# A fifth expert slot from the early plan: attention, a dense layer and routed experts on one Trainium2 core

## The chip, the cores and the metric

The kernel runs on one core of a Trainium2 chip. The metric is the device time of one execution in microseconds (us); a kernel is given by the median of several executions. The engines are named as in the profile: PE (matrix products), DVE and ACT (vector and scalar work), POOL (here mostly the issue of indirect and padding DMAs), SP (here only the issue of DMAs, in the order of its queue; SPq in the rows).

## The reference

Three layers follow one another, in float32.

```python
# 1. gated linear attention, B=4, H=8, S=768, D=48
f = sigmoid(f_logit)
state = f[t] * state + outer(k[t], v[t]);  y[t] = q[t] @ state
# 2. dense layer on the 3072 tokens (width 384, hidden 2048)
h = x @ w_in;  g = softplus(h);  x = g @ w_out
# 3. one expert of eight for each token (hidden 1024)
logits = x @ w_gate + modality_bias[modality_id]
e_idx = argmax(logits);  gate_w = softmax(logits)[e_idx]
out[mask_e] = gate_w * (relu(x[mask_e] @ w1[e]) @ w2[e])
```

How many tokens go to each expert is known only when the second layer is done. On the reference's own inputs the eight counts are 20, 327, 542, 487, 219, 1097, 167 and 213; of the first seven groups of 384 tokens alone they are 17, 281, 476, 430, 193, 956, 154 and 181.

## The kernel before

**First part.** Attention and the dense layer run together over eight groups of 384 tokens (`ffn`). At the end of each group `route1` and `route2` choose the expert of each token and scatter its row into a DRAM buffer `xs`, where each expert has a region of its own, in the order of arrival. After the eighth group, `tails` and `pad_rows` write 256 padding rows behind each expert's last row: eight DMAs on POOL's queue.

**Expert slots.** The third layer runs over a list `seq` of slots, each of one expert: twelve full slots of 256 tokens (number 0 to 11), then one "pair" slot of two half experts of 64 tokens (12), then two slots of 128 tokens (13 and 14). Which expert and which rows a slot takes is decided on the device. `plan_first` counts after seven groups and gives out whole blocks of 256 rows that are complete by then, up to `NPRE` of them. `plan_rest` counts after all eight groups, takes off what the first plan used, and gives out `NA` more full slots, two halves for the pair, and 128-token slots; with the full ones these make the `NSTAT` entries of the fixed list. Only if the plan needs more entries than `NSTAT` a further branch behind the list is entered (up to `NREST` entries, `more`).

**One slot.** `m_fetch` brings what a slot needs while the slot before it computes: two register loads on SP read expert and row from the plan (L994 and L982), one DMA reads the rows (`m_load`, L984, tile `xr`), and eight DMAs (L1008) read the weights in chunks of 128x768 into tiles `raw`, in the order w1, w2, w1, w2 and so on. ACT casts each chunk into a high part (L1009), DVE makes the low part (L1010). The DMA of the rows stands behind the first two chunks. `m_T` turns the rows (L1097 to L1100). `m_up` makes eight hidden tiles: nine products each (L1115), then ACT's relu `hh` (L1117) and DVE's low part `hl` (L1118). `m_down` makes two output tiles of 24 products each (L1138), ACT scales (L1147) and POOL scatters the rows into `out` (L1148). Full slots take turns in two sets of weight tiles, so slot 4 writes into the tiles of slot 2; there are six `raw` tiles and three `xr` tiles, so slot 4's rows go into the tile of slot 1, which is free when slot 1's two output scatters are through.

**Order.** Each engine works off one fixed list in order. A list scheduler makes the lists when the kernel is built, mostly by program order. The steps `final`, `route2`, `ready` (tails and padding) and `then` (the second plan) are hung onto slots 0, 1, 1 and 2:

```python
seq = [("first", i, 2) for i in range(NPRE)] + [("rest", i, 2 if i < NA else 1) for i in range(NSTAT)]
seq.insert(PAIRAT, ("pair", 0, 1))
more = [("rest", i, 1) for i in range(NSTAT, NREST)]
m_slots(seq, {(0, 3): final, (1, 2): lambda: route2(NG - 1), (1, 4): ready, (2, 2): then, (6, 3): limits})
# in m_load: the first plan's rows don't wait for the last group's scatters (scat) and the padding (pads)
for other in scat + pads:
    if where == "first":
        tc.declare_no_dep(ins, other, reason="rows of the groups ahead")
    else:
        after(ins, other)
```

Of the kernel before, what the change touches and what calls it, by code (L numbers as in the profile page):

```python
# [24 lines left out]
NB = 16  # L25
SLOT = 256
CAP = NT + SLOT
NPRE = 4
NA = 8
NREST = 17  # L30
NSTAT = 10
HALF = 64
PAIRAT = 12
LEAN = 16
# [17 lines left out]
def moe_chain(ctx, tc, qT, kT, fT, vp, w_in, w_out, mod, w_gate, mbias, w1, w2, out):  # L52
# [682 lines left out]

    used = cp.tile([NREST, 8], F32, name="used")

    def pick(nm, num, w, offs):


        end, beg, oh, tmp, off = (cp.tile([NREST, w], F32, name=f"{x}{nm}") for x in ("end", "beg", "soh", "stmp", "off"))
        sel, row = (cp.tile([NREST, 1], F32, name=f"{x}{nm}") for x in ("sel", "row"))
        woff, roff = (cp.tile([NREST, 1], I32, name=f"{x}{nm}") for x in ("woff", "roff"))
        nc.vector.tensor_tensor_scan(end, num, zer[:, 0:w], 0.0, op0=ALU.add, op1=ALU.add)
        nc.vector.tensor_tensor(beg, end, num, op=ALU.subtract)
        nc.vector.tensor_scalar(tmp, beg, snum[:, 0:1], None, op0=ALU.is_le)
        nc.vector.scalar_tensor_tensor(oh, end, snum[:, 0:1], tmp, op0=ALU.is_gt, op1=ALU.mult)
        nc.vector.tensor_tensor(tmp, oh, etab[:, 0:w], op=ALU.mult)
        nc.vector.tensor_reduce(sel, tmp, axis=AX.X, op=ALU.add)
        nc.vector.tensor_copy(woff, sel)  # L750

        nc.vector.scalar_tensor_tensor(off, beg, snum[:, 0:1], step[:, 0:w], op0=ALU.subtract, op1=ALU.mult)
        nc.vector.tensor_tensor(tmp, offs, off, op=ALU.subtract)
        nc.vector.tensor_tensor(tmp, tmp, oh, op=ALU.mult)
        nc.vector.tensor_reduce(row, tmp, axis=AX.X, op=ALU.add)
        nc.vector.tensor_scalar(roff, row, float(PADROW), None, op0=ALU.add)
        return woff, roff, beg, end

    def counts(sh, add):
        p = ps_r.tile([128, 512], F32, tag="r", name="r")  # L760
        nc.tensor.matmul(p[:, 0:8], onesb, runb, start=True, stop=True)
        cf, ci = cp.tile([NREST, 8], F32, name=f"cf{sh}"), cp.tile([NREST, 8], I32, name=f"ci{sh}")
        nc.vector.tensor_copy(cf, p[0:NREST, 0:8])
        nc.vector.tensor_scalar(ci, cf, float(add), None, op0=ALU.add)
# [3 lines left out]
    def taken(dst, beg, num, n):  # L768

        nc.vector.tensor_scalar(dst, beg, -1.0, float(n), op0=ALU.mult, op1=ALU.add)  # L770
        nc.vector.tensor_scalar(dst, dst, 0.0, None, op0=ALU.max)
        nc.vector.tensor_tensor(dst, dst, num, op=ALU.min)

    def plan_first():

        _, ci, _ = counts(8, 0)
        num = cp.tile([NREST, 8], F32, name="num0")
        nc.vector.tensor_copy(num, ci)
        woff, roff, beg, _ = pick("0", num, 8, rows0[:, 0:8])
        taken(used, beg, num, NPRE)  # L780
        return woff, roff
# [30 lines left out]
    def plan_rest():  # L812
# [12 lines left out]
        nc.vector.tensor_tensor(beg, end, num, op=ALU.subtract)  # L825
        taken(n16[:, 0:8], beg, num, NA)
        nc.vector.tensor_tensor(num, used, n16[:, 0:8], op=ALU.add)
# [11 lines left out]
    def limits():  # L839
# [4 lines left out]
        nc.vector.tensor_copy(nsl[:, 0:1], end)  # L844
        nc.vector.tensor_scalar(far, end, float(-NSTAT), 0.0, op0=ALU.add, op1=ALU.max)
        nc.vector.tensor_reduce(flm, fl, axis=AX.X, op=ALU.max)
# [34 lines left out]
    def at(s, f):  # L881
        extra.setdefault(s, []).append(f)
# [98 lines left out]
    def m_load(s, where, i, n):  # L981
        ro = nc.sync.value_load(plans[where][1][i:i + 1, 0:1], min_val=0, max_val=PADROW)  # L982
        xr = xrp.tile([128, 2, RW], F32, tag="xr", name="xr")[:, 0:n, :]
        ins = nc.sync.dma_start(xr, xs[bass.ds(ro, 128 * n), :].rearrange("(p j) w -> p j w", j=n)).ins  # L984
# [5 lines that stand above are left out]
        sl[s] = {"xr": xr, "n": n}  # L990
# [164 lines left out]
# [4 lines that stand above are left out]
    plans = {}  # L1159
# [33 lines left out]
    def m_fetch(s, it):  # L1193
        where, i, n = it
        if where == "pair":
            ops = p_weights(s, w2)
            op = ops[2]
            ops[2] = lambda: (p_load(s), op())
            return ops
        ops = m_weights(s, plans[where][0], i, n == 1)  # L1200
        if s not in sl:
            op = ops[2]
            ops[2] = lambda: (m_load(s, where, i, n), op())
        return ops
# [9 lines left out]

    def pre():
        plans["first"] = plan_first()
        for i in range(NPRE - 1):
            m_load(i, "first", i, 2)
        for n, op in enumerate(m_fetch(0, seq[0])):
            at(16 * (NG - 1) + PRE + 1 + n, op)  # L1220
# [7 lines left out]
    rawp = raw0 = pool("raw0", 2, side="right")  # L1228
    m1p = {0: pool("m1a", side="right")}
    at(16 * (NG - 1) + PRE, pre)  # L1230
    ffn(16 * (NG - 1) + 3, ns)
    fi.release()
# [157 lines left out]
    with tc.If(rare > 0):  # L1390
        nv = nc.values_load(nsl[0:1, 0:1], min_val=0, max_val=NREST)
        with tc.If(nv > NSTAT):
            more = [(len(seq) + x, it) for x, it in enumerate(more)]
# [53 lines left out]
```

## Time and profile before

| | |
|---|---|
| median of 3 runs (lowest to highest) | 816.93 us (815.72 to 817.48) |
| the profiled execution | 814.61 us |
| its span, first to last instruction | 812.9 us |
| PE busy | 786.5 us, 97% of the span |
| DVE, ACT, POOL busy | 78%, 65%, 8% |

The profiled execution is one more run, a little below the three others; its span leaves out what lies before the first and behind the last instruction. Busy time of PE counts matrix products that overlap in its pipeline, so 97% says that PE seldom stood still, and not that it runs at its peak.

### The profile page before, as it was taken

The page shows a single profiled execution, that of the slowest core. Times are in us where ns is not written, and L with a number is a line of the kernel's source. Part 1 is how long each engine was busy: PE and PEld are TensorE (multiplying, and loading weights), DVE is VectorE, ACT ScalarE, POOL GpSimd, SP SyncE. Part 2 cuts the span into 40 slices and gives each one's busy share as a digit, 9 for nine tenths or more (in the row PEclk, how much of TensorE's full clock was granted, in tenths as well). Part 3 has the DMA queues.
Part 4 walks back from the last instruction along what each step waited for, and adds up shares of the span by engine and source line. Part 5 has one row for each costly group of instructions (what it writes and reads, how often), then busy time and mean ns, then how long its engine had stood idle before and what let it go on. Part 6 is the DMA issues. An engine that isn't in the chain of part 4 may idle for free.

```text
span 812.9 us, 16010 instructions
## 1 busy us (share of the span) xinstructions
PE 786.5 (97%) x5878; PEld 730.8 (90%) x5878; DVE 633.5 (78%) x1265; ACT 530.4 (65%) x1057; POOL 64.9 (8%) x86
## 2 busy tenths in 40 slices
PE   4899999999999999999999999999999999999997
PEld 4656568999999999999999999989999999999987
DVE  6899999998888888888888866888886766666131
ACT  5787797767766676777676665566775656655242
POOL 2000000200010010010010010100042111000010
PEclk9999999999999999999999999999999999999999
DMA  8794221321132132122221010055598976673980
GB/s 292 255 328 140 59 67 44 91 73 54 45 95 58 45 98 58 51 85 61 62 75 38 23 38 8 30 161 171 200 352 298 309 226 216 213 225 119 366 311 16
DMA packets 53976, 110.84 MB, mean 136 GB/s; under 512 B 7655, under 2 KB 27930, under 8 KB 53888
## 3 DMA queue, kind: packets, MB, share of 16 engines
q1 hardware_dynamic: 48768, 96.61, 37.2%
q0 software_dynamic: 4160, 12.67, 4.2%
q8 instruction: 48, 0.79, 0.4%
q10 hardware_dynamic: 960, 0.44, 0.2%
q14 instruction: 40, 0.33, 0.1%
HBM read 91.92 MB, written 13.65 MB: 130 GB/s over the span
## 4 chain that ended last, share of the span: by engine, by line
PE 49%; DVE 23%; ACT 10%; issue 10%; DMA 7%; SPq 1%; POOL 1%; POOLq 0%; DVEq 0%; ACTq 0%
PE x2ps L653 11%; PE h L573 11%; PE x2ps L1138 10%; PE h L1115 10%; DVE l L637 3%; DVE w L636 2%; DMA raw<-in_w_dram 2%; ACT e L633 1%; DVE f L110 1%; PE r L206 1%; ACT e L622 1%; DVE lo L640 1%; DVE am L214 1%; DVE l L639 1%; ACT r L623 1%
## 5 line engine op out<-in xcount | busy, mean ns | idle before, releaser
L573 PE MATMUL h<-xh,wih 128*128 128x384 f32 x336 | 118.4, 352 | 1.2 <-DVE e L587 1.2
L653 PE MATMUL x2ps<-woh,hi 128*128 128x392 f32 x336 | 115.3, 343 | 1.8 <-ACT hi L612 1.5
L653 PE MATMUL x2ps<-wol,hi 128*128 128x392 f32 x336 | 114.5, 341 | 0.0
L573 PE MATMUL h<-xh,wil 128*128 128x384 f32 x336 | 113.5, 338 | 0.0
L653 PE MATMUL x2ps<-woh,lo 128*128 128x392 f32 x336 | 113.4, 341 | 0.0
L573 PE MATMUL h<-xl,wih 128*128 128x384 f32 x336 | 113.3, 337 | 0.0
L1115 PE MATMUL h<-thl,w1h 128*128 128x256 f32 x528 | 96.5, 284 | 0.0
L1010 DVE TENSOR_TENSOR w2l<-raw,w2h 128x768 fp32r<-128x768 f32 x56 | 53.2, 951 | 38.8 <-ACT w2h L1009 18.0
L1115 PEld LDWEIGHTS h<-thl,w1h 128*128 128x128 f32 x528 | 82.0, 190 | 0.0
L638 ACT CAST hi<-l 128x768 fp32r<-128x768 f32 x48 | 40.0, 834 | 54.1 <-DVE l L637 42.5
L1115 PE MATMUL h<-thl,w1l 128*128 128x256 f32 x264 | 74.3, 282 | 0.0
L1138 PE MATMUL x2ps<-w2h,hh 128*128 128x384 f32 x208 | 71.0, 341 | 0.2 <-ACT rows L679 0.2
L1138 PE MATMUL x2ps<-w2h,hl 128*128 128x384 f32 x208 | 70.1, 337 | 0.8 <-DVE hl L1118 0.8
L1138 PE MATMUL x2ps<-w2l,hh 128*128 128x384 f32 x208 | 69.9, 336 | 0.0
L573 PEld LDWEIGHTS h<-xh,wih 128*128 128x128 f32 x336 | 63.0, 188 | 4.9 <-DVE e L587 2.0
L724 POOL DMA_INDIRECT xs<-rows,pos x24 | 27.1, 1129 | 504.4 <-DVE w L635 166.3
L653 PEld LDWEIGHTS x2ps<-woh,hi 128*128 128x128 f32 x336 | 63.0, 188 | 3.2 <-ACT hi L612 2.6
L653 PEld LDWEIGHTS x2ps<-woh,lo 128*128 128x128 f32 x336 | 63.0, 188 | 0.5
L573 PEld LDWEIGHTS h<-xl,wih 128*128 128x128 f32 x336 | 63.3, 188 | 0.0
L653 PEld LDWEIGHTS x2ps<-wol,hi 128*128 128x128 f32 x336 | 63.1, 188 | 0.0
L573 PEld LDWEIGHTS h<-xh,wil 128*128 128x128 f32 x336 | 63.0, 188 | 0.0
L1010 DVE TENSOR_TENSOR w1l<-raw,w1h 128x768 fp32r<-128x768 f32 x48 | 45.8, 954 | 21.9 <-ACT w1h L1009 21.3
(275 smaller groups left out, 1826.7 us busy)
## 6 DMA issues: line engine op xcount, KB each, us to landing
raw<-in_w_dram SPq DMA_DIRECT2D x104, 384.0 KB
f<-in_f_dram SPq DMA_DIRECT2D x28, 192.0 KB
k<-in_k_dram SPq DMA_DIRECT2D x28, 192.0 KB
q<-in_q_dram SPq DMA_DIRECT2D x28, 192.0 KB
xr<-xs SPq DMA_DIRECT2D x12, 388.0 KB
v<-in_v_dram SPq DMA_DIRECT2D x32, 144.0 KB
w1h<-in_w_dram SPq DMA_DIRECT2D x12, 384.0 KB
xf<-y SPq DMA_DIRECT2D x48, 72.0 KB
```

What stands on the lines that cost most here:

```text
L110: nc.vector.tensor_tensor_scan(d["f"], d["f"], clampt.to_broadcast([128, TG]), 1.0 if first else fl[:, n:n + 1], op0=ALU.mult, op1=ALU.min)
L206: nc.tensor.matmul(pa[h][:, cs], d["k"][64 * h:64 * h + 64, cs], d["q"][64 * h:64 * h + 64, cs], start=(c == 0), stop=True, skip_group_che ...
L214: marks["mask"] = nc.vector.tensor_tensor(am, pa[h][:, 0:TG].rearrange("p (c t) -> p c t", c=3), mask.unsqueeze(1).to_broadcast([128, 3, 1 ...
L573: nc.tensor.matmul(hp, w, x, start=(n == 0), stop=(n == len(terms) - 1))
L636: nc.vector.tensor_tensor(w, w, e, op=ALU.subtract)
L637: nc.vector.tensor_tensor(g, r, g, op=ALU.add)
L638: nc.scalar.copy(hi, g)
L653: nc.tensor.matmul(x2ps[j][:, 0:DM + 8], g[:, ts], w, start=(i == 0 and n == 0), stop=(i == NF - 1 and n == len(terms) - 1))
L724: ins = nc.gpsimd.indirect_dma_start(out=xs, out_offset=bass.IndirectOffsetOnAxis(ap=pos[:, j:j + 1], axis=0), in_=rows[:, j, :], in_offse ...
L1010: nc.vector.tensor_tensor(lo[:, c], t, hi[:, c].bitcast(F32), op=ALU.subtract)
L1115: nc.tensor.matmul(hp[:, 0:SLOT], w[:, kd, fs], t[x][:, kd, :], start=(n == 0), stop=(n == 8))
L1138: nc.tensor.matmul(acc[:, 0:DM], g[:, f, ts], w[:, f, :], start=(f == 0 and n == 0), stop=(f == NF2 - 1 and n == 2))
```

## The change

The first plan gives out five slots in place of four, the plan of the rest seven full ones in place of eight, and the fixed list takes nine of its entries in place of ten. The row count of the plan's small tiles goes from 17 to 18. The rows of slots 0 to 2 are still loaded ahead by `pre`; its loop, which ran to `NPRE - 1`, now has the 3 written out.

```
-NPRE = 4
-NA = 8
-NREST = 17
-NSTAT = 10
+NPRE = 5
+NA = 7
+NREST = 18
+NSTAT = 9
...
     def pre():
         plans["first"] = plan_first()
-        for i in range(NPRE - 1):
+        for i in range(3):
             m_load(i, "first", i, 2)
```

## Rows read from the trace of the kernel before

**Rows 1.** The page: span, and busy time of PE.

```profile
span 812.9 us, 16010 instructions
PE 786.5 (97%) x5878; PEld 730.8 (90%) x5878; DVE 633.5 (78%) x1265; ACT 530.4 (65%) x1057; POOL 64.9 (8%) x86
```

**Rows 2.** Waits of PE, whole span: total us, times, longest.

```profile
PE r L133 <- DVE wih_raw L283: 10.2, 1, 10.2
...
PE x2ps L1138 <- DVE hl L1118: 0.8, 1, 0.8
```

**Rows 3.** Windows of slots 3 and 4: length, busy by engine, PEclk, DMA share, GB/s.

```profile
616.67:635.23 18.56, 17.77 (x127) 17.44 (x127) 12.63 (x20) 11.97 (x22) 2.18 (x2) 1.00 0.99 346
635.23:652.87 17.64, 17.64 (x128) 17.60 (x127) 12.82 (x20) 12.06 (x22) 1.96 (x2) 1.00 0.88 301
```

**Rows 4.** Chain that ended last, 610 to 636: start, us, what.

```profile
619.00 6.66 DMA raw<-in_w_dram
...
625.69 0.03 ACT w1h L1009
...
626.43 0.38 ACT hh L1117
...
628.37 0.73 DVE w2l L1010
...
629.23 0.62 DVE w1l L1010
...
630.10 0.43 DVE hl L1118
...
630.57 0.44 PE x2ps L1138
```

**Rows 5.** Waits of SP's queue, 600 to 618.

```profile
SPq L1026 <- DVE sel L749: 13.8, 1, 13.8
```

**Rows 6.** Timeline of SP's queue, 600 to 618: start, us, issues.

```profile
614.75 0.92 SPq L1008 DMA_DIRECT2D raw<-in_w_dram  x2
616.73 0.33 SPq L984 DMA_DIRECT2D xr<-xs  x1
617.33 0.93 SPq L1008 DMA_DIRECT2D raw<-in_w_dram  x2
```

**Rows 7.** Timeline, 600 to 615, of DVE and PE: start, us, instruction.

```profile
600.45 0.96 DVE L1010 TENSOR_TENSOR w2l<-raw,w2h 128x768 fp32r<-128x768 f32 x1 [1.23 <-ACT w2h L1009]
...
602.86 0.14 DVE L763 COPY cf<-r 17x8 f32<-17x8 f32 x1
...
608.09 0.34 PE L1138 MATMUL x2ps<-w2h,hh 128*128 128x384 f32 x1
...
614.32 0.14 DVE L756 TENSOR_SCALAR roff<-row 17x1 int32<-17x1 f32 x1
```

**Rows 8.** Timeline of POOL, 600 to 613.

```profile
600.16 2.90 POOL L1209 DMA_DIRECT2D xs<-padt  x4 [6.69 <-DMA xs<-rows,pos]
...
608.46 0.68 POOL L1209 DMA_DIRECT2D xs<-padt  x1 [0.80 <-issue]
...
611.49 1.02 POOL L1148 DMA_INDIRECT out_dram<-o,xr  x1 [0.30 <-issue]
```

**Rows 9.** The output scatters, 560 to 700: from issue to landing.

```profile
DMA to landing us min/median/max: 2.5/4.3/7.3
```

**Rows 10.** DMA queues, 597 to 605: packets, MB, share of 16 engines.

```profile
q1 hardware_dynamic: 664, 1.79, 58.7%
q0 software_dynamic: 339, 1.23, 42.2%
```

**Rows 11.** DMA share in tenths, 612 to 617, in 40 slices of 0.125.

```profile
DMA  7831000068985000000000098883019964158798
```

**Rows 12.** Timeline of PE and POOL at the end.

```profile
807.15 0.34 PE L1138 MATMUL x2ps<-w2h,hl 128*128 128x384 f32 x1
...
808.39 0.98 POOL L1148 DMA_INDIRECT out_dram<-o,xr  x1 [8.57 <-ACT o L1147]
```

## The prediction, made before the changed kernel was run

> **What bounds the kernel now.** I read the page first: PE is busy for 786.5 of 812.9 us [rows 1], so anything that does not shorten PE's list or a wait of PE is worth nothing. The table of waits, kept to PE, says where PE waits at all: the longest is 10.2 us for the first attention inputs, and of those within the expert slots the longest is 0.8 us, once, for DVE's `hl` [rows 2]. Windows cut at the first up product of each slot give its place: slot 3 lasts 18.56 us and slot 4, with the same products, 17.64 us [rows 3]. The difference, 0.92 us, is that wait and the slower restart of PE's pipeline. From there PE runs without a gap to its last product at 807.15, and only the last output scatter follows [rows 12].
>
> The chain of work shows what made `hl` late. It enters PE at 630.57 from the last `hl` of slot 3, issued at 630.10. In front of this stand, in the fixed order of DVE and ACT, low and high parts of slot 4's weights, and those waited for a weight chunk: 6.66 us of DMA up to 625.69 [rows 4]. Products of slot 3 are thus held up by preparations for slot 4 that stand ahead of them in the queue.
>
> SP's queue says why those chunks were late. Between 600 and 618 it has one long wait, 13.8 us, for the second plan's `sel` [rows 5]. (The instruction is a register load for the pair, drawn forward in the list; slot 4's own loads of expert and row stand behind it and need the same plan.) The first two chunks of slot 4 go out from 614.75, the rows at 616.73, the other six chunks from 617.33 [rows 6]. The plan itself runs on DVE from 602.86 to 614.46 between other work [rows 7].
>
> **The change, part by part.** *The list.* From the reference's counts, blocks of 256 that are complete after seven groups number 0, 1, 1, 1, 0, 3, 0, 0 by expert: six, so a fifth exists. Before, the first plan gives experts 1, 2, 3, 5 and the rest 2, 3, 4, 5, 5, 5, 6, 7; after, 1, 2, 3, 5, 5 and 2, 3, 4, 5, 5, 6, 7. The twelve full slots are the same blocks in another order, the pair (experts 0 and 2) and the two 128-token slots (1 and 5) stay, and the rest fills exactly nine entries, so the further branch stays closed. PE's work: 0. Had the fifth block not been full, a slot of padding would have cost 17.64 us [rows 3]; the counts exclude it.
>
> *The small tiles* get 18 rows for 17. An instruction on them takes 0.14 us [rows 7]; more rows add no elements to a row, so 0. Were time in proportion to rows, some 40 instructions by 0.14/17 would make 0.3 us of DVE, which lies under PE's products and is no longer awaited in slot 3. *The loop of `pre`* makes the same three loads: 0.
>
> *Slot 4 from the first plan.* Its register loads need nothing from the second plan, so SP can issue its first two chunks when `raw` tiles come free. The conversions that free them run from 600.45 [rows 7], so I put the two issues at about 602 to 604, some 12 us earlier. Behind them stands the DMA of slot 4's rows, and here a new wait appears: no longer for the plan, but for the `xr` tile of slot 1, whose last output scatter POOL issues only at 611.49, behind the eight padding DMAs [rows 8]. All later chunks are queued behind it on SP, and the casts on ACT and the low parts on DVE behind them.
>
> When is that tile free? In the DMA share, a burst ends at 613.6 and the next, which follows the scatter after it, begins at 614.9 [rows 11]; so I give the scatter of 611.49 the shortest landing, 2.5 us: 614.0. The bounds are the median and the longest, 4.3 and 7.3 us [rows 9]: 615.8 and 618.8. To each I add what the two early chunks take from the padding: a chunk is 384 KB, or 393,216 bytes, and at the 346 GB/s of slot 3's window [rows 3] 1.14 us, for two 2.3 us. From 597 to 605 the two queues together fill the DMA engines, 58.7% and 42.2% [rows 10], so I take the whole 2.3 us and not nothing. That gives 616.3 for the rows, with bounds from 614.0 (no shift, shortest) to 621.1 (full shift, longest).
>
> Against 616.73 before, the rows leave 0.4 us earlier. In addition, the stream behind them carries two chunks less, 2.3 us. So the six remaining chunks land about 2.7 us earlier, and with them the casts in front of `hh` and `hl`. The last `hl` of slot 3 was 0.8 us late [rows 2], so the stall goes with 1.9 us to spare: **-0.92 us** [rows 3].
>
> The Trainium skill, in "DMA: Bandwidth & Descriptors", section "Queues, rings and completion order", says that each DMA engine takes its queue rows in turn, packet by packet. By that rule the two early chunks share the engines with the padding instead of filling a gap, which speaks against the change: the output scatter behind the padding lands later. The trace agrees as far as the two shares of 58.7% and 42.2% show it; by the rule the sum is the same as mine, and without it the rows would leave 2.3 us earlier still.
>
> *What becomes late next.* The first conversion of slot 4 needs slot 2's w1 tiles, free when its up products end, shortly before its first down product at 608.09 [rows 7]; its w2 tiles are free when slot 3 begins, at 616.67 [rows 3]. So at most one low part of 0.95 us [rows 7] lands among the plan's instructions. It makes the plan later by as much: ready at about 615.4. The plan's next user is slot 5's register loads, which SP reaches after slot 4's eight chunks, at about 622; some 6 us cover it. Without that cover each us of plan would delay slot 5's chunks by one.
>
> *The wait for scatters and padding* falls away for slot 4's rows: 0, since these DMAs are issued by 608.46 [rows 8] and the tile's wait ends later. The longer further branch is not entered: 0.
>
> **Sum.** The profiled execution took 814.61 us, so 814.61 - 0.92 = 813.69. It lies 2.32 us under the median of the three runs, 816.93, so carried to that median: 816.93 - 0.92 = **816.0 us**, or 0.11% less. From no change the measurement tells about 0.2%, 1.6 us: the forecast is "the same".
>
> **Rivals.** *The stall stays: 816.9 us.* The change frees a wait, but PE's order decides. If the scheduler leaves SP's early register load for the pair ahead of slot 4's chunks, or puts more conversions ahead of `hl`, the 0.92 us remain. For it speaks that this very load stands ahead now [rows 5]; against it, that slot 4's loads are ready long before the plan. 0.18.
>
> *Slower: the `xr` tile comes free too late, 819.0 us.* The place is SP's issue of slot 4's rows. It decides when that comes later than 616.73 + 2.3 = 619.0, since then the six chunks land later than now in spite of the lighter stream. At the bound of 621.1, 2.1 us later, slot 3 grows by 2.1 us: 816.9 + 2.1. For it speaks that POOL issues the padding first; against it, the gap in the DMA share from 613.6 to 614.9 [rows 11], by which the tile would be free well before. 0.08.
>
> *Slower in another place: 817.8 us.* A new order of the lists lets PE wait once more, by one such stall of 0.92 us, and keeps the old one. Nothing points to a place: from slot 4 on PE waits nowhere. 0.07.
>
> *Faster by more: 815.1 us or less.* Behind the eight groups PE has no second stall of this size to give back, so only a luckier order could, by as much again. 0.05.
>
> **How the numbers follow.** The forecast keeps 0.62. Its own range is the spread of the runs, about 0.9 us to each side: 815.1 to 816.9. To hold 8 in 10 the range takes in the stall that stays and, with the same spread, the second stall's lower half: 814.8 to 818.0; left out are the slow rival with 0.08, part of the third, and the low end of the fast one. Faster by over 0.2% is below 815.3: a sixth of the forecast by spread and nearly all of the last rival, 0.14. Slower is above 818.6: the `xr` rival and a little of the third, 0.09. The same: 0.77.
>
> **What would show it.** Right: slot 4's first two chunks leave SP around 602 to 604; its rows leave between 614 and 617, after slot 1's scatter; slot 3's window shrinks to about 17.6; PE's wait for `hl` is gone; the second plan's result is awaited by nobody on PE's path. Wrong: slot 4's first chunk still leaves after 613; its rows leave after 619; or a window from slot 1 to slot 5 grows by half a us and more. A time away from 816 by more than 1.6 us with these windows unchanged would mean that the cause lies in the part before the slots or at the end, where I expect nothing to move.

## The result: slower by 0.8%

The changed kernel takes 823.26 us (median of 6 runs, 822.48 to 825.08), the kernel before, on the same chip, 816.97 us (6 runs, 815.72 to 817.63). The ratio is 1.008, with a 95% interval from 1.0066 to 1.0094. The forecast was 816.0 us, in a range up to 818.0: it was wrong, and on the side to which it had given 0.09.

The page of the kernel after, beside [rows 1]: the instructions are as many as before, PE's busy time is only 2.2 us longer, but the span grew by 9.1.

```profile
span 822.0 us, 16010 instructions
...
PE 788.7 (96%) x5878; PEld 732.4 (89%) x5878; DVE 633.6 (77%) x1265; ACT 530.3 (65%) x1057; POOL 63.6 (8%) x86
```

The table of PE's waits, beside [rows 2]. The wait of 0.8 us for `hl` in slot 3's down products is gone, as forecast. A wait of 6.0 us, for `hl` too but in the up products, stands in the second place of the list.

```profile
PE r L133 <- DVE wih_raw L283: 10.3, 1, 10.3
PE h L1115 <- DVE hl L1118: 6.0, 1, 6.0
```

Windows of slots 3 and 4, beside [rows 3]:

```profile
617.29:642.87 25.58, 19.60 (x127) 19.36 (x127) 14.49 (x27) 12.81 (x23) 2.18 (x2) 0.87 0.82 263
642.87:660.52 17.65, 17.65 (x128) 17.61 (x127) 11.17 (x18) 10.75 (x20) 2.02 (x2) 1.00 0.74 234
```

Slot 3 takes 25.58 us where it took 18.56: 7.02 us more, and that is the difference of the medians (6.29) and a little over. Slot 4 takes what it took. Of the 9.1 us by which the spans of the two profiled executions differ, 0.62 us lie ahead of slot 3, where profiled executions vary anyway (slot 3 starts between 615.62 and 620.90 in those of this document), and 1.4 us at the end: from the end of PE's last product (815.19, before 807.49) to the end of the span it is 6.8 us where it was 5.4. Against an undisturbed 17.65 us slot 3 loses 7.93: PE is idle for 25.58 - 19.60 = 5.98 us, and its products take 1.95 us longer. The same slot cut in four shows both parts (the eighth figure is PEclk):

```profile
617.29:621.40 4.11, 4.11 (x36) 4.11 (x36) 0.00 (x0) 0.71 (x1) 0.00 (x0) 1.00 0.99 298
621.40:624.85 3.45, 0.30 (x3) 0.10 (x1) 1.58 (x7) 0.71 (x2) 0.00 (x0) 1.00 0.98 352
624.85:631.65 6.80, 3.96 (x18) 3.96 (x19) 6.27 (x11) 5.78 (x12) 1.09 (x1) 0.50 0.60 193
631.65:642.87 11.22, 11.22 (x74) 11.18 (x73) 6.63 (x10) 5.61 (x10) 1.09 (x1) 1.00 0.85 265
```

PE runs 36 products, the four up groups for which it has `h` buffers, and stops at 621.4. In the first 4.11 us ACT does 0.71 us of work and DVE nothing at all: nobody empties the buffers. While PE stands, its granted clock falls to half (the 1.2 GHz level), and the first 4 us of products after the stall run at that.

What ACT did instead, from its timeline (start, us, instruction, and in brackets the idle time before it and its releaser):

```profile
609.29 0.84 ACT L1009 CAST w1h<-raw 128x768 fp32r<-128x768 f32 x1 [0.86 <-DMA raw<-in_w_dram]
610.03 0.38 ACT L1117 ACTIVATE hh<-h 128x256 fp32r<-128x256 f32 x1
...
620.69 0.84 ACT L1009 CAST w1h<-raw 128x768 fp32r<-128x768 f32 x1 [6.77 <-DMA raw<-in_w_dram]
624.27 0.83 ACT L1009 CAST w1h<-raw 128x768 fp32r<-128x768 f32 x1 [2.74 <-DMA raw<-in_w_dram]
...
626.21 0.39 ACT L1117 ACTIVATE hh<-h 128x256 fp32r<-128x256 f32 x1
```

The relu at 626.21 is slot 3's first. In ACT's list the casts of slot 4's second and third w1 chunk now stand ahead of it, and both wait for their DMA. (So do slot 2's last output scaling and slot 4's first w2 cast, between 625.01 and 626.21.) In the kernel before only the first w1 cast stood ahead of slot 3's first relu; the second and third stood between the relus:

```profile
618.18 0.84 ACT L1009 CAST w1h<-raw 128x768 fp32r<-128x768 f32 x1 [0.72 <-DMA raw<-in_w_dram]
618.92 0.38 ACT L1117 ACTIVATE hh<-h 128x256 fp32r<-128x256 f32 x1
...
622.40 0.84 ACT L1009 CAST w1h<-raw 128x768 fp32r<-128x768 f32 x1 [0.89 <-DMA raw<-in_w_dram]
...
625.69 0.84 ACT L1009 CAST w1h<-raw 128x768 fp32r<-128x768 f32 x1 [1.16 <-DMA raw<-in_w_dram]
```

The Trainium skill, in "PSUM — Partial Sum Buffer", section "Engine vs sequencer instructions", says that the queues of ScalarE, VectorE and GpSimdE are strictly first in, first out. The trace agrees: the relu at 626.21 did not pass the casts, though its products were done before 621.40.

SP's and POOL's timelines, beside [rows 6] and [rows 8]: SP issues slot 4's first two chunks at 602.05 and 603.25 (they are two of the first three), the rows at 616.32, and then slot 4's other six chunks (the eight of the third line take in two of slot 5). POOL issues slot 1's last scatter at 613.03.

```profile
600.17 3.41 SPq L1008 DMA_DIRECT2D raw<-in_w_dram  x3
616.32 0.33 SPq L984 DMA_DIRECT2D xr<-xs  x1
616.90 10.76 SPq L1008 DMA_DIRECT2D raw<-in_w_dram  x8
```

```profile
611.52 1.21 POOL L1148 DMA_INDIRECT out_dram<-o,xr  x1 [0.30 <-issue]
613.03 1.02 POOL L1148 DMA_INDIRECT out_dram<-o,xr  x1 [0.30 <-issue]
```

The chain of work of this stretch ties it together, beside [rows 4]: scatter, SP's rows, a chunk, ACT, DVE's `hl`, PE.

```profile
613.03 3.16 DMA out_dram<-o,xr
616.32 0.33 SPq L984
...
618.07 6.17 DMA raw<-in_w_dram
...
625.58 0.73 ACT w2h L1009
...
627.21 0.43 DVE hl L1118
...
627.69 4.40 PE h L1115 x20
```

### The profile page after: what moved, and what is told of

The parts are those of the page before. It is cut to its first block, busy times and chain, and to the rows that moved or that the text cites. A ratio compares the mean times of both kernels' runs of the same rounds, so it can differ in the third digit from the quotient of the medians.

```text
span 822.0 us, 16010 instructions
## 1 busy us (share of the span) xinstructions
PE 788.7 (96%) x5878; PEld 732.4 (89%) x5878; DVE 633.6 (77%) x1265; ACT 530.3 (65%) x1057; POOL 63.6 (8%) x86
## 4 chain that ended last, share of the span: by engine, by line
PE 48%; DVE 18%; issue 16%; ACT 8%; DMA 6%; POOL 1%; POOLq 1%; SPq 1%; DVEq 0%; ACTq 0%
PE h L573 13%; PE x2ps L653 13%; PE h L1115 8%; PE x2ps L1138 8%; DVE l L637 2%; PE r L206 2%; DVE w L636 2%; DVE f L110 1%; DMA f<-in_f_dram 1%; PE r L182 1%; PE r L194 1%; DMA xf<-y 1%; DVE am L214 1%; ACT e L633 1%; POOL out_dram L1148 1%
## 5 line engine op out<-in xcount | busy, mean ns | idle before, releaser
L1115 PE MATMUL h<-thl,w1h 128*128 128x256 f32 x528 | 98.4, 287 | 6.0 <-DVE hl L1118 6.0
```

What stands on the lines that cost most here:

```text
L1115: nc.tensor.matmul(hp[:, 0:SLOT], w[:, kd, fs], t[x][:, kd, :], start=(n == 0), stop=(n == 8))
```

## The experiments

Two theories stood after this. *Late chunks alone*: slot 4's chunks come too late for slot 3, because of the `xr` wait or the padding's traffic. *Order times late chunks*: the scheduler, which sees that slot 4's loads need no plan, lists their casts ahead of slot 3's relus; that costs only as much as the chunks behind those casts are late. In the diffs `follow` fixes an order in an engine's list without a wait. The experiments are told in the order of the argument; 1, 3, 4 and 8 were made first, when I put the loss on late chunks behind the `xr` wait (theory A of their expectations).

**1. The early fetch taken back, the five planned slots kept.** Slot 4's first chunk waits for the second plan again.

```diff
-                    nc.sync.dma_start(t, rows)
+                    ins = nc.sync.dma_start(t, rows)
+                    if s == 4 and n == 0 and src is w1:
+                        after(ins.ins, plan_done[0])
```

> The changed kernel, but slot 4's first weight chunk is made to wait for the last instruction of the second plan, as it did before; experts, rows and plan sizes are those of the change. Theory A: the lists of ACT are then those of the kernel before, slot 3 lasts about 18.5 us, time 816.9, 1.000 of before. Rival E (the other experts' weights and rows, the 18 rows of the plan's tiles, or the longer spare branch cost the time): it stays at 823.

Measured: 815.93 us, ratio to before 1.0005 (0.9981 to 1.0028); slot 3 takes 18.99 us, and ACT's list in slot 3 is that of before.

```profile
615.62:634.61 18.99, 17.78 (x128) 17.45 (x127) 12.63 (x20) 12.08 (x22) 2.18 (x2) 1.00 0.99 348
```

The other order of experts, the eighteenth row and the further branch cost nothing that can be measured (the interval leaves room for 0.28%, or 2.3 us). The loss comes with the early fetch.

**2. The kernel before with the new order.** Four planned slots, chunks behind the second plan as ever; only slot 3's first four relus are put behind the cast of slot 4's third w1 chunk.

```diff
-            nc.scalar.activation(d["hh"][:, f, :], hp[:, 0:SLOT], AF.Relu)
+            ins = nc.scalar.activation(d["hh"][:, f, :], hp[:, 0:SLOT], AF.Relu)
+            if s == 3 and f < 4:
+                follow(ins, marks["w1", 4, 2])
...
+            if s == 3:
+                for _ in range(5):
+                    wops.pop(0)()
```

> The kernel before, with its four planned slots, but with the list order of the kernel after in one place: slot 3's first four relus on ACT stand behind slot 4's cast of w1 chunk 2. The chunks still wait for the second plan on SP and land from about 622 on. Theory 'order of the lists times late chunks' (ACT's list puts slot 4's casts ahead of slot 3's relus, and the chunks behind those casts are late): slot 3 grows by 6 to 8 us, the time is 823 to 825 us, although nothing of the change is in the kernel. Rival 'the early fetch itself costs it, through DMA traffic and the xr wait' (the order is harmless): slot 3 stays under 20 us and the time is at most 818 us.

Measured: 822.11 us, ratio 1.006 (1.004 to 1.008). Slot 3's window, and ACT's timeline in it:

```profile
618.34:643.40 25.06, 20.72 (x128) 19.91 (x127) 14.91 (x22) 13.90 (x24) 1.96 (x2) 0.86 0.87 294
```

```profile
624.88 0.83 ACT L1009 CAST w1h<-raw 128x768 fp32r<-128x768 f32 x1 [2.99 <-DMA raw<-in_w_dram]
...
627.24 0.84 ACT L1009 CAST w1h<-raw 128x768 fp32r<-128x768 f32 x1 [0.31 <-DMA raw<-in_w_dram]
627.99 0.65 ACT L1117 ACTIVATE hh<-h 128x256 fp32r<-128x256 f32 x2
```

Nothing of the change is in this kernel, and slot 3 loses nearly what it loses after it: 6.50 us against 7.02. The order alone, with chunks as late as they always were, is enough; the time was 1 us under what I had expected.

**3 and 4. The `xr` wait taken away.** In the one, slot 4's rows have a tile of their own (two `o` buffers less make the room); in the other they are issued behind the seventh chunk.

```diff
-        xr = xrp.tile([128, 2, RW], F32, tag="xr", name="xr")[:, 0:n, :]
+        xr = (gp.tile([128, 2, RW], F32, tag="xr4", name="xr4") if s == 4 else
+              xrp.tile([128, 2, RW], F32, tag="xr", name="xr"))[:, 0:n, :]
```

```diff
-            op = ops[2]
-            ops[2] = lambda: (m_load(s, where, i, n), op())
+            k = 6 if s == 4 else 2
+            op = ops[k]
+            ops[k] = lambda: (op(), m_load(s, where, i, n)) if s == 4 else (m_load(s, where, i, n), op())
```

> The changed kernel, but slot 4's rows get a tile of their own, so that their DMA has no output scatter to wait for (two of the fifteen output tiles are given up for the space). Theory A (the DMA of slot 4's rows stands on SP from about 604 to 616 waiting for slot 1's output scatter, six weight chunks stand behind it, and casts of these chunks stand ahead of slot 3's relus in ACT's list): the wait on SP goes, the chunks arrive before the casts are due, PE's 6.0 us wait in slot 3 goes, slot 3 lasts 17.6 to 18.0 us, time 816.0, or 0.999 of before. Rival B (the new order of ACT's list costs by itself, whenever the chunks come): the 6 us stay, about 823. Rival C (the early chunks crowd the padding DMAs and that delays something on PE's path): more chunks go early here, so 823 or more.

> The changed kernel, but the DMA of slot 4's rows is issued behind its seventh weight chunk in place of its second; the row tile is still slot 1's. Theory A: seven chunks leave SP without waiting for slot 1's scatter, the rows leave at about 616 to 618 as now and are needed only at the seventh up product of slot 3, about 624; no stall in slot 3, 816.0 to 816.5, 0.999 of before. Rival B (order alone): 823. Rival D (late rows, and not late chunks, hold PE): the rows are as late as now, so 823.

Measured: 821.41 us (ratio 1.0067, 1.0044 to 1.0091) and 820.26 us (1.0058, 1.0035 to 1.008); slot 3 takes 24.68 and 22.29. With the tile SP waits no more: rows at 602.73, the chunks from 603.76. ACT waits all the same:

```profile
602.73 0.79 SPq L985 DMA_DIRECT2D xr<-xs  x1
603.76 14.00 SPq L1009 DMA_DIRECT2D raw<-in_w_dram  x6
```

```profile
615.58 0.84 ACT L1010 CAST w1h<-raw 128x768 fp32r<-128x768 f32 x1 [5.56 <-DMA raw<-in_w_dram]
...
619.68 0.83 ACT L1010 CAST w1h<-raw 128x768 fp32r<-128x768 f32 x1 [3.26 <-DMA raw<-in_w_dram]
```

A chunk issued at 603.76 is there only at 615.58. Slot 3 is 0.90 and 3.29 us shorter than in the kernel after, of the 7.02 us that it had lost. So the wait, on which I had put the whole loss at first, is less than half of it; the times of the two kernels are too near to that of the kernel after, for their intervals, to say more. Without the wait the chunks run in one stream with the padding, which POOL issues from 599.73 to 611.29. Both edits also moved the list: slot 4's fourth w1 cast, which in the kernel after follows slot 3's second relu, now stands ahead of the first (at 621.68 and 620.85). The two figures are thus not the price of the wait alone.

**5 to 7. Half the padding.** 128 rows behind each expert's rows in place of 256 (no slot reads more), in the kernel after, in the kernel with the tile, and in the kernel before as a control.

```diff
-        ins = nc.gpsimd.dma_start(xs[bass.ds(r, SLOT), :].rearrange("(p j) w -> p j w", j=2),
-                                padt.unsqueeze(1).to_broadcast([128, 2, RW])).ins
+        ins = nc.gpsimd.dma_start(xs[bass.ds(r, 128), :], padt).ins
```

> The kernel after with 128 rows of padding written behind each expert's rows in place of 256, so half the bytes; no slot reads beyond the 128. Theory 'the chunks are late because SP waits for the output scatter behind the padding and the padding fills the DMA engines': the scatter of slot 1 leaves POOL no later, lands earlier, the rows of slot 4 leave SP by 612 to 613 and the six chunks land by 622 to 623; slot 3 shrinks from 25.6 to 19 to 21 us, time 817 to 818.5 us. Rival 'padding bytes do not matter, only the instructions of POOL that issue it': rows still leave at about 616, time 823 us.

> The kernel after with both causes of late chunks taken away: slot 4's rows in a tile of their own (no wait for slot 1's output scatter) and half the bytes of padding. Theory 'order of the lists times late chunks, and these two make them late': chunks land before slot 3's relus need the casts, slot 3 is 17.6 to 18 us, time 816.0 us. Rival 'padding is not what holds the chunks up once the wait for the tile is gone': as with the tile alone, slot 3 about 24.7 us, time 821 us.

> The kernel before with 128 rows of padding written behind each expert's rows in place of 256: a control for the runs with short padding. The padding lies under PE's products in the kernel before, so 816.9 us, no change. If short padding costs time by itself (the kernel after with short padding took 827 us), 819 to 821 us.

Measured: 826.13 us (three runs; 1.0126, 1.0102 to 1.0149), 818.41 us (1.003, 1.0011 to 1.0049), and 816.83 us for the control (1.0004, 0.9988 to 1.002). The theory fell for the first: the rows leave SP at 616.30, and slot 3 takes 25.75 us. Counted from POOL's first padding DMA, which comes 1.8 us later than in the kernel after (602.47 against 600.65), slot 1's last scatter leaves after 11.08 us in place of 12.38 and the rows after 13.83 in place of 15.67. So, by these two executions, half the bytes take less than 2 us off the wait for the `xr` tile, which is mostly not a matter of bytes. Here too the fourth w1 cast (625.77) has moved ahead of slot 3's first relu, which starts 8.54 us into the slot. Why this kernel is slower still than the kernel after (1.0126 against 1.008) is open: of the 2.1 us between the spans of the two profiled executions, 0.2 lie in slot 3 and 1.9 ahead of the first padding DMA, which the edit does not touch. With the tile as well, the bytes do count: slot 3 falls from the 24.68 us of the tile alone to 19.90. That lies between the two expectations, since some casts still wait for their chunk, 3.83 us at 616.79 and 0.83 us at 621.53; the latter is the fourth w1 cast, ahead of the first relu in this kernel as well.

**8 and 9. The old order put back.** First each cast of slot 4 was only kept behind the relu that was traced last:

```diff
-                    nc.scalar.copy(hi[:, c], t)
+                    ins = nc.scalar.copy(hi[:, c], t)
+                    if s == 4:
+                        follow(ins, marks["relu"])
```

> The changed kernel, but each cast of slot 4's chunks is put behind the relu of slot 3 that is traced just before it, by an ordering edge without a wait; chunks and rows leave SP as in the changed kernel. Theory A: chunks are as late as now, but no relu stands behind them; slot 3 loses its 6 us or all but 1 us of it, 816.0 to 817.5. Rival F (the late chunks hold PE by themselves, by slot 4's start): 821 or more, with the wait moved to the first products of slot 4.

Measured: 823.25 us (1.0078, 1.0052 to 1.0103), so the expectation of 816.0 to 817.5 fell. The stall moved into slot 3's down products, where PE waits 6.7 us for `hh`; slot 3 takes 27.34.

```profile
PE x2ps L1140 <- ACT hh L1119: 6.7, 1, 6.7
```

Slot 3's first relu now starts 1.31 us into the slot, but its last, at 639.95, stands behind two casts of slot 4 that wait 3.50 and 2.62 us for their chunks (635.28 and 639.21). Then slot 4's operations were also spread over slot 3's groups as the kernel before has them:

```diff
-                if wops:
+                for _ in range({0: 2, 3: 1, 4: 1, 5: 1, 6: 1, 7: 2}.get(f, 0) if s == 3 else bool(wops)):
```

> The kernel after, but each cast of slot 4 is held behind the latest relu of slot 3, one or two operations for each relu, so that ACT's list has the order of the kernel before; slot 4's fetch stays early in the list of SP. Theory 'order of the lists times late chunks': no relu of slot 3 waits for a cast of a late chunk, slot 3 is 17.6 to 18.6 us and the time 816.0 to 816.9 us. Rival 'late chunks alone' (the chunks of slot 4 come too late whatever the order): slot 3 stays above 23 us and the time at or above 821 us.

Measured: 822.27 us (1.006, 1.0038 to 1.0082). Windows of slots 3 and 4, and the register loads by line (durations in ns, then first and last start):

```profile
617.61:635.11 17.50, 17.50 (x128) 17.46 (x127) 11.58 (x18) 11.49 (x21) 0.99 (x2) 1.00 0.79 252
635.11:659.90 24.79, 20.10 (x127) 19.86 (x127) 14.54 (x23) 12.85 (x23) 3.15 (x3) 0.86 0.85 269
```

```profile
L994 SPq TENSOR_LOAD <-woff x6: 264/266/279, 619.4 to 625.6; - x6
```

Slot 3 is healed, as the order theory says, and not by earlier chunks. But slot 4 now loses the same 7 us. Between slot 4's sixth and seventh chunk SP's list holds six loads of `woff` and six of `roff`, for six later slots, from 619.44 to 626.75: 7.3 us, 0.61 us for each. So slot 5's chunks are late, and ACT's list for slot 4 has casts first. The run before this one has the same block, from 623.8 to 631. The Trainium skill, in "DMA: Bandwidth & Descriptors", section "Latency and other measured facts", gives some 600 ns as the floor of a register load. The trace agrees as far as the spacing goes, 0.61 us from load to load; the load by itself stands there with 0.27 us.

**10 to 13. The old order without the block of loads.** Slots 6 and up read expert and row from copies that DVE makes behind a relu's `hl`, so that SP cannot load them long ahead. (A block of six loads, for slot 5 and the pair, remains: in experiment 12 from 620.77 to the next chunk at 624.87.) In the first pair a slot's copy stands behind the last `hl` of the slot two ahead of it, in the second pair three ahead. In each pair the second kernel also has the tile and the short padding.

```diff
+        if where == "rest" and s >= 6:
+            t = cp.tile([NREST, 2], I32, tag="late", name="late", bufs=2)
+            for x in (0, 1):
+                follow(nc.vector.tensor_copy(t[:, x:x + 1], plans["rest"][x]), marks["hl"])
+            plans[s] = [t[:, 0:1], t[:, 1:2]]
+            where = s
```

```diff
-                follow(nc.vector.tensor_copy(t[:, x:x + 1], plans["rest"][x]), marks["hl"])
+                follow(nc.vector.tensor_copy(t[:, x:x + 1], plans["rest"][x]), marks["hl", min(s - 3, 11)])
```

> The kernel after with slot 4's casts held behind slot 3's relus as in the run before it, and in addition the expert and row of slots 6 and up read from copies that DVE makes only after the relus of the slot ahead, so that SP's list has no block of twelve register loads between slot 4's chunks (that block took 7.3 us, from 619.44 to 626.75, in the run before it). Theory 'order of the lists times late chunks': with ACT's order of the kernel before, and chunks that land as in the kernel after, slots 3 and 4 take 17.6 to 18.6 us each, time 816.0 to 817.0 us. Rival 'late chunks alone': a slot of 3 to 5 stays above 21 us and the time at or above 820 us. Rival 'the stall of slot 4 came from something else than the register loads': slot 3 is 17.6, slot 4 above 20 us, time 819 to 822 us.

> The same with, in addition, slot 4's rows in a tile of their own and 128 rows of padding for each expert in place of 256, so that no wait of SP and less traffic stands before slot 4's chunks. If the order of the lists was all that was left, this equals the run beside it, 816.0 to 816.5 us, slot 3 at 17.6 us and no wait of PE within the slots; if early chunks are worth something by themselves, it is faster than the kernel before by the 0.9 us of slot 3's stall and more, 815.0 to 816.0 us; if the early traffic costs something by itself, it is slower than 818 us.

Measured: 822.43 us (1.0075, 1.0045 to 1.0104) and 824.13 us (1.0085, 1.0055 to 1.0115). Slots 3 and 4 take 17.60 and 17.63 us, then 17.58 and 17.61, so the stalls are gone from both. But my copies came too late for the slots behind: slots 5 to 10 take 109.96 us together in the first kernel and 112.16 in the second, and took 105.64 before.

> As the run with copies of the plan (after, slot 4's casts behind slot 3's relus, expert and row of slots 6 and up read from copies), but each copy is made one slot earlier: in that run slots 3 and 4 took 17.60 and 17.63 us, and slots 5 to 10 lost 4.5 us to the late copies. Theory 'order of the lists times late chunks, and SP's block of register loads as the second way to the same stall': slots 3 to 11 now take what they took before, with slot 3 at 17.6 us, time 816.0 us. Rival 'the early fetch costs something beside the two': some slot stays above 19 us or the time above 818.5 us.

> The same with slot 4's rows in a tile of their own and 128 rows of padding for each expert. Theory as beside: equal to the run beside it, 816.0 us, since chunks on time buy nothing that the order has not bought already. If chunks that land early are worth something by themselves: under 815.5 us.

Measured: 816.24 us (1.0006, 0.9989 to 1.0024) and 815.62 us (0.9999, 0.9984 to 1.0013). Slots 3 and 4 of the first:

```profile
618.48:636.08 17.60, 17.60 (x127) 17.57 (x127) 12.57 (x21) 12.12 (x22) 1.09 (x2) 1.00 0.94 323
636.08:653.71 17.63, 17.63 (x127) 17.59 (x127) 13.31 (x24) 12.08 (x22) 3.15 (x3) 1.00 0.85 282
```

```profile
619.79 0.39 ACT L1119 ACTIVATE hh<-h 128x256 fp32r<-128x256 f32 x1 [0.52 <-PE h L1117]
620.07 0.83 ACT L1009 CAST w1h<-raw 128x768 fp32r<-128x768 f32 x1
...
626.71 0.83 ACT L1009 CAST w1h<-raw 128x768 fp32r<-128x768 f32 x1 [0.31 <-DMA raw<-in_w_dram]
```

The early fetch, the `xr` wait (rows at 618.04) and the full padding are all in this kernel; the third w1 cast comes as late as ever, 8.2 us into slot 3 (7.0 in the kernel after). Beside the copies only the lists differ, and the loss is gone; slots 5 to 10 take 105.8 us together. Chunks that land earlier, in the second kernel, buy nothing that can be told. Neither beats the kernel before, though slot 3 is 0.96 us shorter there. The profiled executions show where about as much goes: from PE's last product to the end of the span it is 6.2 and 6.3 us in these two kernels, from 6.1 to 6.8 us in all twelve kernels that hold the change, and from 5.4 to 5.6 us in the three that do not (the kernel before, experiments 2 and 7). Which part of the change does this no run takes apart.

Over the runs, slot 3's loss goes with one number, how long after slot 3's first product ACT gets to its first relu. The exception is experiment 8, where the last relu was held up and not the first:

| kernel | first relu, us into slot 3 | slot 3, us |
|---|---|---|
| old order, copies in time | 1.31 | 17.60 |
| after, casts behind the relu traced last (experiment 8) | 1.31 | 27.34 |
| before | 2.25 | 18.56 |
| after, early fetch taken back | 2.30 | 18.99 |
| after, tile and short padding | 3.13 | 19.90 |
| after, rows behind the seventh chunk | 5.39 | 22.29 |
| after, tile alone | 7.38 | 24.68 |
| after, short padding | 8.54 | 25.75 |
| after | 8.92 | 25.58 |
| before, casts first | 9.65 | 25.06 |

## Why the prediction was wrong, point by point

- *The list of slots, the eighteenth row, the branch: 0.* Right as far as the time can tell: with the early fetch taken back 1.0005. But the prediction expected nothing to move at the end, and there the kernels with the change take 0.5 to 1.4 us longer behind PE's last product; that is as much as the 0.92 us that were to be won.
- *First two chunks out at 602 to 604.* Right: 602.05 and 603.25.
- *The new wait: rows out at 616.3.* Right: 616.32. The way there was partly luck: the scatter left POOL 1.5 us later than in the kernel before (613.03 against 611.49) and landed in 3.16 us, where the sum had 2.3 and 2.5; the two errors nearly cancel.
- *The six chunks land about 2.7 us earlier.* Nearly: counted from slot 3's first product, the second w1 cast starts 3.40 us in (5.73 before), the third 6.98 (9.02): 2.0 to 2.3 us earlier.
- *"... and with them the casts in front of `hh` and `hl`. ... so the stall goes".* **This step failed.** It took the casts in front of the relus from the list of the kernel before. They were not the same ones: the second w1 cast had stood behind four of slot 3's relus and the third behind six, and now both stand ahead of the first. The old stall did go, and one of 6.0 us came in its place: the term of -0.92 us for slot 3 came out as +7.02. Experiment 2 shows that this order alone makes the loss, experiment 12 (old order, copies in time) that all the rest of the change without this order makes none that can be measured.
- *At most one low part lands among the plan's instructions; plan ready at about 615.4.* Both are wrong, for the same reason: two low parts of slot 4 stand there, at 610.86 and 621.57, since in the new lists its second w1 conversion comes ahead of the plan's end as well. That one waits on DVE for its cast, and the plan waits behind it, until 623.08. Slot 5's register loads on SP then wait 0.3 us for the plan, and PE waits nowhere in slot 4:

```profile
610.86 0.94 DVE L1010 TENSOR_TENSOR w1l<-raw,w1h 128x768 fp32r<-128x768 f32 x1
...
615.05 0.15 DVE L749 TENSOR_REDUCE sel<-stmp 18x1 f32<-18x16 f32 x1
621.57 0.96 DVE L1010 TENSOR_TENSOR w1l<-raw,w1h 128x768 fp32r<-128x768 f32 x1 [6.37 <-ACT w1h L1009]
...
623.08 0.14 DVE L756 TENSOR_SCALAR roff<-row 18x1 int32<-18x1 f32 x1
```

- *The rivals.* "The stall stays" named the mechanism, more conversions ahead of `hl`, but priced it at the old 0.92 us, as if one more cast could only cost what the present ones cost. "Slower in another place" said that nothing points to a place. Something did: slots 5 and on have their next slot's w1 casts ahead of the relus, which costs them nothing as their chunks are there. A slot 4 that needs no plan could be expected to be scheduled like them, but its chunks were to leave SP only at 616.3, by my own sum. The price could have been read: the third w1 cast had waited until 625.69 [rows 4], 9.0 us into slot 3; with 2.7 us off that, a first relu behind it starts more than 6 us into the slot, where it had started at 2.25. The condition of the `xr` rival, rows later than 619.0, did not come about.
- *The rule of the Trainium skill on queues taken in turn* ("DMA: Bandwidth & Descriptors", section "Queues, rings and completion order"). It spoke against the change. The runs agree as far as the sharing goes: with the tile a chunk issued beside the padding takes 11.8 us from issue to cast (603.76 to 615.58); half the padding on top of the tile brings slot 3 from 24.68 to 19.90. In the kernel after the wait for the tile hid this.

## What to carry to other kernels

When a fetch is freed from a wait, ask not only when its data now land but where the scheduler will put the work on them. Here one dependency more (experiment 1) or less moved the casts of one slot behind or ahead of another slot's relus, presumably because the scheduler lists by the arrival it believes in, which no run shows directly. An in-order engine then holds back work that was ready behind data that are not there. Price such an order by the arrival of the last piece ahead of the critical instruction, not by the stall that is there now. If the fetch is to be early, fix the order of the lists as well, and look at every engine's list afterwards: an order fixed on ACT moved twelve register loads on SP.

## What the runs showed of the hardware that was not expected

A stall of PE can cost more than its length. In the kernel after, PE stood from 621.4 and its granted clock was half (the 1.2 GHz level) from 624.85 for 6.8 us. In that stretch 18 products took 3.96 us, where 36 had taken 4.11 at the slot's start; this is nearly all of the 1.95 us that came on top of 5.98 us of idle time. With the tile alone PE stood from 616.8, and the clock was half from 620.0 for 6.8 us. In the kernel with the rows behind the seventh chunk, whose longest gap was 2.15 us, the clock stayed full in slot 3; there too the products took longer, by 1.06 us (18.71 against 17.65), so the clock is not the only thing that a broken stream of products costs.
